# Two places for converted weights, and low parts kept in the raw buffer, in the first MoE of an attention kernel

## The chip, the cores and the metric

One core of one Trainium2 chip runs the whole program. The metric is the device time of one execution in microseconds (us); the kernel before takes 2153.35 us, the median of three runs (2152.96 to 2153.58). The engines are TensorE (PE, its weight loads PEld), VectorE (DVE), ScalarE (ACT), GpSimd (POOL) and SyncE (SP), which issues all the DMAs here. Each engine works through its own instructions in the order in which the program gave them out, and waits on semaphores for the others.

## The reference, cut to what matters

Attention with random features gives 2304 tokens of 512 numbers. They go through a first MoE (three weight matrices), and its result through a second with eight experts:

```python
g = x @ w_gate                       # 512 x 1536
silu = g * (1.0 / (1.0 + np.exp(-g)))
val = x @ w_val                      # 512 x 1536
x = (silu * val @ w_out)             # 1536 x 512
...
for e in range(E):                   # second MoE: w1[e] 512 x 1024, w2[e] 1024 x 512
    h = np.maximum(x @ w1[e], 0.0)
    out += P[:, e:e + 1] * (h @ w2[e])
```

The three weight matrices of the first MoE arrive as 64-bit floats, everything else as 32-bit floats. A product keeps its precision by splitting both factors in a high part (a rounded copy) and a low part (the rest), with three matmuls: high times high, high times low, low times high.

## The kernel before, in words

The program has three stages that matter here: attention (to 178 us), the first MoE (178 to 668 us), the second MoE (the rest).

**First MoE** (`moe1`). Six groups `g` of 256 hidden columns; in each, six steps `b` of 384 tokens. A step gives out `hunit(g, b, 0)`, then `ounit` of the step before, then `hunit(g, b, 1)`: 24 matmuls each (L707 to L709 in hunit, L739 to L741 in ounit), 72 in a step. At its end a hunit turns its two PSUM banks into the high and low part that the ounit will multiply: ACT silu (L717), DVE product (L718), ACT rounded copy (L721), DVE rest (L722). An ounit adds its four banks into an accumulator on DVE (L746).

**Weight tasks** (`m1_task`). The weights of group g+1 are made beside the matmuls of group g by six tasks, two for each matrix. A task is a generator: `pump(1)` runs it to its next `yield`, so that its instructions lie between those of the matmuls. Before the change a task has these pieces: ACT makes a float of the low word (L183); DVE has five operations on 32-bit words (L185, L187, L189, L191, L193) with two scratch halves of the tile `cv`, `a` and `s`; POOL multiplies (L195) and adds (L197); after an empty piece ACT makes the high part (L200) and POOL the low part (L202). That is 11 pieces. The load of a later task (L167 or L171, 512 KB, on SP) follows when the next pump finds the task at its end; it writes the raw buffer that the finished task has read. A step calls `pump(1)` ten times: three in each hunit, four in the ounit. After the ounit of a group's first step, `flush` runs whatever is left of the six tasks in one go, and the next six are put in the queue. From that queue's first pump to the flush there are 3 + 5 x 10 + 3 + 4 = 60 calls. The first six tasks run in the attention stage, at two pumps a step of its loop (L195 to L202 there too); L465 is the low part of the attention's input on DVE, L515 a matmul that reads it, and L436 the load of that input on SP.

**Sums** (`sums`). A second generator, `side`, makes sums of the second MoE's w2 blocks for later. It is called 14 times in a step: five times in each hunit, four in the ounit. For each of 32 blocks it loads 512 KB into one of two raw buffers (L306, SP), forms four sums on POOL in place (`subs`, L311 to L314), and for each half c makes a high part on ACT (L332, 128x512) and a low part on DVE (L338), and writes both to memory with four DMAs (L320, SP). Before the change there is one place for the high part and one for the low, `hl[0]` and `hl[1]`, so a half can be rounded only when the writes of the half before have landed. A block has 12 pieces; 14 pieces come ahead of the first block.

The generators give the order: nothing is moved about by a scheduler, and a semaphore wait stands wherever an instruction needs what another engine or a DMA has made, or writes what another still reads.

Of the kernel before, what the change touches and what calls it, by code (L numbers as in the profile page):

```python
# [11 lines left out]
F32 = mybir.dt.float32  # L12
F32R = mybir.dt.float32r
AF = mybir.ActivationFunctionType
ALU = mybir.AluOpType
# [5 lines left out]
P = 128  # L21
# [25 lines left out]
def f(ap):  # L47
    return ap.bitcast(F32)


class Kernel:
# [47 lines left out]
    def flush(self):  # L99
        while self.bg:  # L100
            self.pump(1000)

    def enqueue(self, n):
        for _ in range(n):
            self.bg.append(self.task(self.ntask))
            self.ntask += 1
# [28 lines left out]

    def make_tasks(self):
        self.tasks, self.raws, self.ntask, self.done = [], {}, 0, set()
        self.ahead, self.nload, self.tags, self.writes = 2, 0, deque((0, 1)), deque()
        for g in range(NG1):
            for which in range(3):  # L140
                for i in range(2):
                    self.tasks.append(self.m1_task(g, which, i))
        o = len(self.tasks) + 2
        for m in range(NG2):
            for q in range(2):
                self.tasks.append(self.w1_task(m, q))
            for i in range(2):
                self.tasks.append(self.w2_task(m, i))
        self.tasks.insert(o, self.tasks.pop(o + 2))
# [6 lines left out]
    def m1_task(self, g, which, i):  # L156
        nc = self.nc
        src = (self.wg, self.wv, self.wo)[which]
        dt, w = (F32, 1) if src.dtype == F32 else (I32, 2)
        if w == 2:  # L160
            src = src.bitcast(I32)
        src = src.rearrange("r (c w) -> r c w", w=w)

        def load(tag):
            if which < 2:
                t = self.raw.tile([P, 2, 256, w], dt, tag=tag, name=f"m1raw{g}_{which}_{i}")
                nc.sync.dma_start(t, src[i * 256:(i + 1) * 256, g * 256:(g + 1) * 256, :].rearrange("(c p) f w -> p c f w", p=P))  # L167
                return t.rearrange("p c f w -> p (c f) w")
            t = self.raw.tile([P, 512, w], dt, tag=tag, name=f"m1raw{g}_{which}_{i}")
            r0 = g * 256 + i * P  # L170
            nc.sync.dma_start(t, src[r0:r0 + P, :, :])  # L171
            return t

        def ops(t):
            hi, lo = [x.rearrange("p a b -> p (a b)")[:, i * 512:(i + 1) * 512] for x in self.m1_weights(g, which)]
            if dt == F32:
                x = t[:, :, 0]
            else:
                v = nc.vector
                w0, w1 = t[:, :, 0], t[:, :, 1]  # L180
                a, s = self.cv[:, 0:512], self.cv[:, 512:1024]
                x, y = f(a), t[:, :, 0].bitcast(F32)
                nc.scalar.activation(y, w0.bitcast(U32), AF.Copy, scale=2.0 ** -52)  # L183
                yield
                v.tensor_scalar(a, w1, 0x7FFFFFFF, None, op0=ALU.bitwise_and)  # L185
                yield
                v.tensor_scalar(x, x, F64_LO, F64_HI, op0=ALU.max, op1=ALU.min)  # L187
                yield
                v.tensor_scalar(a, a, 3, 0x3FFFFFF8, op0=ALU.logical_shift_left, op1=ALU.bitwise_and)  # L189
                yield  # L190
                v.scalar_tensor_tensor(a, w1, -0x40000000, a, op0=ALU.bitwise_and, op1=ALU.bitwise_or)  # L191
                yield
                v.tensor_scalar(s, a, -0x800000, None, op0=ALU.bitwise_and)  # L193
                yield
                nc.gpsimd.tensor_tensor(y, y, f(s), op=ALU.mult)  # L195
                yield
                nc.gpsimd.tensor_tensor(x, x, y, op=ALU.add)  # L197
                yield
                yield
            nc.scalar.copy(hi, x)  # L200
            yield
            nc.gpsimd.tensor_tensor(lo, x, f(hi), op=ALU.subtract)  # L202
            yield

        return load, ops, ("m1", g, which, i)


# [87 lines left out]

    def sums(self):
        nc, g_ = self.nc, self.nc.gpsimd
        hl = [self.ar2[:, 3072 + x * 512:3584 + x * 512] for x in range(2)]
        raws = [self.raw.tile([P, 2, 512], F32, tag="raw2", name="sumsraw"), self.cst.tile([P, 2, 512], F32, tag="ar2b", name="sumsraw2")]
        order = [(m, k) for m in range(NG2) for k in range(2)]  # L300

        def load(i):
            m, k = order[i]
            e, g = divmod(m, 2)
            r0 = g * 512 + k * 256
            nc.sync.dma_start(raws[i % 2], self.w2[e, r0:r0 + 256, :].rearrange("(c p) f -> p c f", p=P))  # L306

        def subs(i):
            t = raws[i % 2]
            a11, a21, a12, a22 = t[:, 0, 0:256], t[:, 0, 256:512], t[:, 1, 0:256], t[:, 1, 256:512]  # L310
            g_.tensor_tensor(a22, a21, a22, op=ALU.add)  # L311
            g_.tensor_tensor(a21, a11, a21, op=ALU.subtract)
            g_.tensor_tensor(a11, a22, a11, op=ALU.subtract)
            g_.tensor_tensor(a12, a12, a11, op=ALU.subtract)  # L314

        def write(i, c):
            m, k = order[i]
            for x in range(2):
                for j, n in enumerate(((6, 7), (3, 5))[c]):
                    nc.sync.dma_start(self.w2f[:, m, self.USE2.index(n), k, x, :], f(hl[x][:, j * 256:(j + 1) * 256]))  # L320

        load(0)
        for _ in range(8):
            yield
        subs(0)
        for _ in range(6):
            yield
        for i in range(len(order)):
            t = raws[i % 2]
            more = i + 1 < len(order)  # L330
            for c in range(2):
                nc.scalar.copy(hl[0], t[:, c, :])  # L332
                if c == 0 and more:
                    load(i + 1)
                yield
                if c and more:
                    subs(i + 1)
                nc.vector.tensor_tensor(hl[1], t[:, c, :], f(hl[0]), op=ALU.subtract)  # L338
                yield
                yield  # L340
                write(i, c)
                for _ in range(3):
                    yield

    def run(self):
        tc, nc = self.tc, self.nc
# [1162 lines left out]
```

## Time and profile before

| | |
|---|---|
| median of 3 runs | 2153.35 us (2152.96 to 2153.58) |
| the profiled execution | 2158.95 us, of which its span is 2157.2 us |
| PE busy | 2083.8 us, 97% of the span |
| DVE, POOL, ACT busy | 1361.2, 1055.9, 825.5 us (63%, 49%, 38%) |
| mean granted TensorE clock | 0.988 of full speed |
| read and written in memory | 337.89 and 125.35 MB |

The span runs from the first to the last instruction of one profiled execution. A busy share is a mean over all stages. A wait is idle time of an engine, put down to the semaphore event that came last before it ended. The granted clock is 1 at 2.4 GHz and 0.5 at 1.2 GHz.

### The profile page before, as it was taken

The numbers are of one execution on the slowest core, as the hardware profiler recorded it, in microseconds if no ns is written. First come the engines' busy times: TensorE is split into PE (matmuls) and PEld (weight loads), VectorE is DVE, ScalarE is ACT, GpSimd is POOL, SyncE is SP. The second block draws the span as 40 slices with busy tenths as digits, with TensorE's granted clock in tenths as the row PEclk, the third lists the DMA queues.
The fourth block names the chain that finished last, engine by engine and source line by source line (L and its number), as shares of the span: only waits on it lengthen the run. The fifth ranks groups of instructions, "written<-read, shape, count | busy, mean of one in ns | idle before, by whom it ended". The sixth has DMA issues, their size and how long they took to land.

```text
span 2157.2 us, 32509 instructions
## 1 busy us (share of the span) xinstructions
PE 2083.8 (97%) x11836; PEld 2008.9 (93%) x11836; DVE 1361.2 (63%) x2319; ACT 825.5 (38%) x1843; POOL 1055.9 (49%) x1049
## 2 busy tenths in 40 slices
PE   7999998998999999999999999999999999999998
PEld 7889998988999899899988999999998999999998
DVE  6996566666555654454445566666667566666666
ACT  6785433333244353344333433333233333333332
POOL 6774655555452454555454434434436434434433
PEclk9999999999999999999999999999999999999999
DMA  6542555555323567657667678877877778877784
GB/s 199 172 153 86 179 179 168 171 166 180 104 79 115 202 241 261 233 213 279 254 232 287 221 261 258 257 257 253 278 265 230 247 258 258 258 257 253 249 266 151
DMA packets 236752, 465.39 MB, mean 216 GB/s; under 512 B 20176, under 2 KB 108976, under 8 KB 232496
## 3 DMA queue, kind: packets, MB, share of 16 engines
q1 hardware_dynamic: 236592, 463.32, 63.9%
q8 instruction: 93, 1.52, 0.3%
q14 instruction: 67, 0.55, 0.1%
HBM read 337.89 MB, written 125.35 MB: 215 GB/s over the span
## 4 chain that ended last, share of the span: by engine, by line
PE 81%; DVE 8%; POOL 3%; ACT 3%; issue 2%; DMA 2%; SPq 0%; DVEq 0%; ACTq 0%; POOLq 0%
PE bank L1052 12%; PE pair L1383 7%; PE bank L1292 7%; PE bank L1294 7%; PE bank L1293 7%; PE pair L1385 7%; PE pair L1384 7%; PE bank L993 3%; PE bank L995 3%; PE bank L994 3%; PE bank L707 3%; PE bank L709 3%; PE bank L708 3%; DMA w2forms<-ar 2%; PE bank L739 2%
## 5 line engine op out<-in xcount | busy, mean ns | idle before, releaser
L1395 DVE TENSOR_TENSOR sums<-pair,sums 128x768 f32<-128x768 f32 x209 | 198.9, 952 | 46.2 <-PE pair L1385 46.1
L1292 PE MATMUL bank<-xh,ar 128*128 128x384 f32 x568 | 190.8, 336 | 4.4 <-DVE sums L1330 1.8
L1293 PE MATMUL bank<-xl,ar 128*128 128x384 f32 x568 | 190.3, 335 | 0.0
L1294 PE MATMUL bank<-xh,ar 128*128 128x384 f32 x568 | 190.3, 335 | 0.0
L1068 DVE SCALAR_TENSOR_TENSOR ac<-bank,mt,ac 128x512 f32<-128x512 f32 x84 | 63.1, 751 | 130.7 <-PE bank L1052 128.9
L195 POOL TENSOR_TENSOR m1raw<-m1raw,cv 128x512 f32<-128x512 f32 x36 | 49.6, 1378 | 171.2 <-issue 105.5
L1383 PE MATMUL pair<-xh,ar 128*128 128x384 f32 x342 | 115.0, 336 | 0.0
L1384 PE MATMUL pair<-xl,ar 128*128 128x384 f32 x342 | 114.6, 335 | 0.0
L1385 PE MATMUL pair<-xh,ar 128*128 128x384 f32 x342 | 114.6, 335 | 0.0
L1292 PEld LDWEIGHTS bank<-xh,ar 128*128 128x128 f32 x568 | 107.2, 189 | 5.7 <-DVE sums L1330 2.2
L1293 PEld LDWEIGHTS bank<-xl,ar 128*128 128x128 f32 x568 | 107.1, 189 | 0.0
L1294 PEld LDWEIGHTS bank<-xh,ar 128*128 128x128 f32 x568 | 107.1, 188 | 0.0
L718 DVE TENSOR_TENSOR mt<-bank,mt 128x384 f32<-128x384 f32 x72 | 40.0, 555 | 98.6 <-ACT mt L717 49.6
L707 PE MATMUL bank<-xh,ar 128*128 128x384 f32 x288 | 96.7, 336 | 0.0
L709 PE MATMUL bank<-xh,ar1b 128*128 128x384 f32 x288 | 96.2, 334 | 0.0
L709 PE MATMUL bank<-xh,ar 128*128 128x384 f32 x288 | 96.2, 334 | 0.0
L708 PE MATMUL bank<-xl,ar 128*128 128x384 f32 x288 | 96.2, 334 | 0.0
L707 PE MATMUL bank<-xh,ar1b 128*128 128x384 f32 x288 | 96.2, 334 | 0.0
L708 PE MATMUL bank<-xl,ar1b 128*128 128x384 f32 x288 | 96.2, 334 | 0.0
L993 PE MATMUL bank<-xh,ar 128*128 128x384 f32 x264 | 89.5, 339 | 6.5 <-DVE mt L1027 3.8
L535 ACT ACTIVATE at<-bank,bi 128x128 f32<-128x128 f32 x288 | 78.6, 395 | 43.1 <-DVE bi L528 36.0
L995 PE MATMUL bank<-xh,ar 128*128 128x384 f32 x264 | 89.0, 337 | 0.1
(382 smaller groups left out, 6958.2 us busy)
## 6 DMA issues: line engine op xcount, KB each, us to landing
ar<-w2forms SPq DMA_DIRECT2D x143, 512.0 KB, 4.5
ar<-w1forms SPq DMA_DIRECT2D x142, 512.0 KB, 4.9
w2forms<-ar SPq DMA_DIRECT2D x352, 128.0 KB, 2.9
ar1b<-w1forms SPq DMA_DIRECT2D x62, 512.0 KB, 4.9
ar1b<-w2forms SPq DMA_DIRECT2D x61, 512.0 KB, 4.4
w1forms<-ar SPq DMA_DIRECT2D x22, 1280.0 KB, 7.0
sumsraw<-in_w_dram SPq DMA_DIRECT2D x32, 512.0 KB, 4.5
w1raw<-in_w_dram SPq DMA_DIRECT2D x32, 512.0 KB, 4.3
```

The lines of the kernel that those rows point to most:

```text
L707: nc.tensor.matmul(t, hi[:, c, fs], self.xh[:, c, cs], start=(c == 0), stop=False)
L708: nc.tensor.matmul(t, hi[:, c, fs], self.xl[:, c, cs], start=False, stop=False)
L709: nc.tensor.matmul(t, lo[:, c, fs], self.xh[:, c, cs], start=False, stop=(c == KC - 1))
L993: nc.tensor.matmul(g, ah[:, c, :], bh[:, c, :], start=(first and c == 0), stop=False, skip_group_check=not first)
L1052: nc.tensor.matmul(y, a, w[:, fi % 2, ds], start=(first and x == 0 and k == 0 and fi == fis[0]), stop=(last and x == 1 and fi == fis[-1]))
L1292: nc.tensor.matmul(g, w[:, 0, d], bh[:, d, :], start=bool(first and d == 0), stop=False, skip_group_check=not first)
L1293: nc.tensor.matmul(g, w[:, 0, d], bl[:, d, :], start=False, stop=False, skip_group_check=not first)
L1294: nc.tensor.matmul(g, w[:, 1, d], bh[:, d, :], start=False, stop=(d == 1), skip_group_check=not first)
L1383: nc.tensor.matmul(y, w[:, k, 0, ds], h, start=(k == 0), stop=False)
L1384: nc.tensor.matmul(y, w[:, k, 0, ds], l, start=False, stop=False)
L1385: nc.tensor.matmul(y, w[:, k, 1, ds], h, start=False, stop=(k == 1))
L1395: v.tensor_tensor(a[n], pair, a[n], op=ALU.add)
```

## The change

Three things are changed. The weight tasks get two places for the converted value: `a` alternates between the halves of `cv`, and `s` goes into the raw buffer, over the high word that nothing reads any more. The split of a converted value (L200 and L202 before) leaves the task and becomes a generator of its own, `late`, which the next task runs: ACT's copy after the next task's L189, POOL's subtraction just ahead of its multiplication; `flush` runs what is left. The multiplication gets an empty piece behind it, and a task has 10 pieces instead of 11. In `sums`, the high parts get two places (one for each half c), the low parts are written over the raw values, and the order of a block's 13 pieces is: copy, subtract, next block's load, write; copy, subtract, empty, write; empty, the four sums of the next block, three empty.

```diff
     def flush(self):
         while self.bg:
             self.pump(1000)
+        for _ in self.late:
+            pass
...
+        def split(x):
+            hi, lo = [w.rearrange("p a b -> p (a b)")[:, i * 512:(i + 1) * 512] for w in self.m1_weights(g, which)]
+            nc.scalar.copy(hi, x)
+            yield
+            nc.gpsimd.tensor_tensor(lo, x, f(hi), op=ALU.subtract)
...
-                a, s = self.cv[:, 0:512], self.cv[:, 512:1024]
+                n = self.nconv % 2
+                self.nconv += 1
+                a, s = self.cv[:, n * 512:(n + 1) * 512], w1
...
                 v.tensor_scalar(a, a, 3, 0x3FFFFFF8, op0=ALU.logical_shift_left, op1=ALU.bitwise_and)
+                next(self.late, None)
                 yield
                 v.scalar_tensor_tensor(a, w1, -0x40000000, a, op0=ALU.bitwise_and, op1=ALU.bitwise_or)
                 yield
                 v.tensor_scalar(s, a, -0x800000, None, op0=ALU.bitwise_and)
                 yield
-                nc.gpsimd.tensor_tensor(y, y, f(s), op=ALU.mult)
+                for _ in self.late:
+                    pass
+                nc.gpsimd.tensor_tensor(y, y, s.bitcast(F32), op=ALU.mult)
+                yield
                 yield
                 nc.gpsimd.tensor_tensor(x, x, y, op=ALU.add)
-                yield
-                yield
-            nc.scalar.copy(hi, x)
-            yield
-            nc.gpsimd.tensor_tensor(lo, x, f(hi), op=ALU.subtract)
-            yield
+                self.late = split(x)
+                yield
+                yield
...
-        hl = [self.ar2[:, 3072 + x * 512:3584 + x * 512] for x in range(2)]
-        raws = [self.raw.tile([P, 2, 512], F32, tag="raw2", name="sumsraw"), self.cst.tile([P, 2, 512], F32, tag="ar2b", name="sumsraw2")]
+        his = [self.ar2[:, 3072 + x * 512:3584 + x * 512] for x in range(2)]
+        raws = [self.raw.tile([P, 2, 512], F32R, tag="raw2", name="sumsraw"), self.cst.tile([P, 2, 512], F32R, tag="ar2b", name="sumsraw2")]
+        lows, raws = raws, [f(r) for r in raws]
...
-            for x in range(2):
+            for x, w in enumerate((his[c], lows[i % 2][:, c, :])):
                 for j, n in enumerate(((6, 7), (3, 5))[c]):
-                    nc.sync.dma_start(self.w2f[:, m, self.USE2.index(n), k, x, :], f(hl[x][:, j * 256:(j + 1) * 256]))
+                    nc.sync.dma_start(self.w2f[:, m, self.USE2.index(n), k, x, :], f(w[:, j * 256:(j + 1) * 256]))
...
             for c in range(2):
-                nc.scalar.copy(hl[0], t[:, c, :])
+                nc.scalar.copy(his[c], t[:, c, :])
+                yield
+                nc.vector.tensor_tensor(lows[i % 2][:, c, :], t[:, c, :], f(his[c]), op=ALU.subtract)
+                yield
                 if c == 0 and more:
                     load(i + 1)
                 yield
-                if c and more:
-                    subs(i + 1)
-                nc.vector.tensor_tensor(hl[1], t[:, c, :], f(hl[0]), op=ALU.subtract)
-                yield
-                yield
                 write(i, c)
-                for _ in range(3):
-                    yield
+                yield
+            yield
+            if more:
+                subs(i + 1)
+            for _ in range(4):
+                yield
```

## Rows read from the trace of the kernel before

**Rows 1.** The page: the span, and busy time of each engine.
```profile
span 2157.2 us, 32509 instructions
PE 2083.8 (97%) x11836; PEld 2008.9 (93%) x11836; DVE 1361.2 (63%) x2319; ACT 825.5 (38%) x1843; POOL 1055.9 (49%) x1049
```

**Rows 2.** Stretches: length, busy PE, PEld, DVE, ACT, POOL (us), granted clock, DMA share, GB/s.
```profile
0.00:177.82 177.82, 153.91 (x1228) 147.36 (x1229) 153.03 (x343) 131.07 (x404) 126.91 (x169) 0.99 0.51 168
177.82:584.85 407.03, 386.89 (x2200) 381.34 (x2198) 257.61 (x434) 139.57 (x273) 220.97 (x212) 0.97 0.50 158
...
667.56:2157.20 1489.64, 1460.26 (x7936) 1398.63 (x7935) 903.99 (x1461) 522.77 (x1100) 676.06 (x644) 0.99 0.72 245
```

**Rows 3.** Same view: single steps of the first MoE, first to next hunit.
```profile
265.47:282.84 17.37, 14.48 (x73) 13.87 (x73) 10.33 (x16) 6.33 (x12) 10.63 (x12) 0.90 0.53 157
...
334.55:347.03 12.48, 12.48 (x74) 12.48 (x73) 9.08 (x16) 3.74 (x7) 7.85 (x8) 1.00 0.46 148
347.03:367.17 20.14, 15.37 (x74) 14.96 (x73) 11.24 (x17) 6.32 (x12) 13.36 (x14) 0.83 0.53 159
...
404.83:418.56 13.73, 13.03 (x73) 12.39 (x73) 10.14 (x18) 4.63 (x9) 7.78 (x8) 1.00 0.70 211
...
514.52:534.68 20.16, 15.17 (x73) 14.76 (x73) 11.04 (x17) 6.44 (x12) 13.24 (x13) 0.83 0.48 148
```

**Rows 4.** Waits of PE from 253 to 585 us: total, times, longest.
```profile
PE bank L739 <- ACT ar L721: 19.2, 7, 5.0
```

**Rows 5.** Timeline, 346 to 358 us: start, length, instruction, idle before it and releaser.
```profile
349.54 0.38 SPq L167 DMA_DIRECT2D m1raw<-in_gate_dram  x1
349.55 0.62 ACT L200 CAST ar<-cv 128x512 fp32r<-128x512 f32 x1 [6.59 <-POOL cv L197]
350.02 8.11 SPq L320 DMA_DIRECT2D w2forms<-ar  x7
...
354.44 0.62 ACT L332 CAST ar<-sumsraw 128x512 fp32r<-128x512 f32 x1 [3.71 <-DMA w2forms<-ar]
354.97 0.48 ACT L717 ACTIVATE mt<-bank 128x384 f32<-128x384 f32 x1
```

**Rows 6.** Busy time by stretch, straight behind the longest wait of that step.
```profile
356.64:362.30 5.66, 5.66 (x18) 5.57 (x19) 5.01 (x9) 1.37 (x3) 2.78 (x2) 0.50 0.46 135
```

**Rows 7.** Busy time: the second step of group 5, sums done, gating matmuls added.
```profile
597.33:611.22 13.89, 13.89 (x81) 13.89 (x81) 8.21 (x16) 7.71 (x16) 9.13 (x9) 1.00 0.20 64
```

**Rows 8.** Waits of ACT, then of SP, from 178 to 585 us.
```profile
ACT ar1b L200 <- POOL cv L197: 52.6, 13, 8.3
ACT ar L200 <- POOL cv L197: 46.4, 12, 8.3
ACT ar L332 <- DMA w2forms<-ar: 36.0, 21, 3.9
...
SPq L167 <- DVE cv L191: 23.2, 4, 6.1
```

**Rows 9.** Lines asked for singly: ns least/median/most; last two: landing of L320, L306.
```profile
L185 DVE TENSOR_SCALAR cv<-m1raw x36: 410/616/960, 23.8 to 591.4; 128x512 int32<-128x512 int32 x36
L191 DVE SCALAR_TENSOR_TENSOR cv<-m1raw,cv x36: 676/682/695, 31.1 to 593.8; 128x512 int32<-128x512 int32 x36
L193 DVE TENSOR_SCALAR cv<-cv x36: 410/417/430, 34.9 to 594.6; 128x512 int32<-128x512 int32 x36
L195 POOL TENSOR_TENSOR m1raw<-m1raw,cv x36: 1295/1302/1764, 35.5 to 595.1; 128x512 f32<-128x512 f32 x36
L338 DVE TENSOR_TENSOR ar<-sumsraw,ar x64: 678/1025/1756, 196.7 to 568.5; 128x512 fp32r<-128x512 f32 x64
...
DMA to landing us min/median/max: 1.7/2.2/4.8
DMA to landing us min/median/max: 3.6/4.5/5.8
```

**Rows 10.** POOL's groups from 178 to 585 us: busy us, mean ns.
```profile
L311 POOL TENSOR_TENSOR sumsraw<-sumsraw 128x256 f32<-128x256 f32 x31 | 28.6, 924 | 0.0
```

More of the change, by code (lines that the diff above doesn't have):

```diff
@@ L137, in make_tasks @@
         self.tasks, self.raws, self.ntask, self.done = [], {}, 0, set()
+        self.late, self.nconv = iter(()), 0
         self.ahead, self.nload, self.tags, self.writes = 2, 0, deque((0, 1)), deque()
@@ L172, in load @@
             return t
+        def split(x):
[3 more added lines that the diff above has]
+            nc.gpsimd.tensor_tensor(lo, x, f(hi), op=ALU.subtract)
         def ops(t):
-            hi, lo = [x.rearrange("p a b -> p (a b)")[:, i * 512:(i + 1) * 512] for x in self.m1_weights(g, which)]
             if dt == F32:
                 x = t[:, :, 0]
+                yield from split(x)
+                yield
             else:
@@ L335, in sums @@
                 yield
-                if c and more:
-                    subs(i + 1)
-                nc.vector.tensor_tensor(hl[1], t[:, c, :], f(hl[0]), op=ALU.subtract)
+                write(i, c)
                 yield
+            yield
+            if more:
+                subs(i + 1)
+            for _ in range(4):
                 yield
-                write(i, c)
-                for _ in range(3):
-                    yield
     def run(self):
```

## The prediction

> **What bounds the kernel now.** First the page: PE is busy for 2083.8 of 2157.2 us [rows 1], so a change that leaves the matmuls alone can only win back PE's idle time and time at a lower clock. Next the stretches, to find the stage: the change touches groups 0 to 4 of the first MoE, 407.0 us with a granted clock of 0.97, and six tasks in attention; the 1489.6 us behind the first MoE hold none of it [rows 2]. Then single steps. An undisturbed step takes 12.48 us, PE busy throughout [rows 3]; 30 of them would take 374.4 us, so 407.03 - 374.4 = 32.6 us are lost here. They are lost in a pattern: the second step of groups 1 to 4 takes 17.4 to 20.2 us (four steps, of which three stand in the rows, 17.37, 20.14 and 20.16), and the sixth step of groups 1 to 3 about 14 us (three steps, one in the rows, 13.73) [rows 3]. PE's waits name the releaser: 19.2 us in seven waits for ACT's rounded copy L721 [rows 4]. That is less than 32.6, since the clock falls after the idle time: the 5.66 us behind the longest wait of one such step ran at 0.50, the 1.2 GHz level [rows 6]. Idle time and half clock go together; what removes one removes the other.
>
> Why L721 is late stands in the timeline of one such step [rows 5]. ACT first sits 6.59 us before L200, the split of the sixth task, because POOL's addition L197 is given out just ahead of it in the flush. It then sits 3.71 us before L332, because the one place for a high part is still being written out: that write was issued at 350.02, behind the load L167 at 349.54, which SP held until L197 had read the raw buffer. Only then comes the silu L717, at 354.97. Both waits are common: 99.0 us in 25 waits before L200 and 36.0 us in 21 before L332 [rows 8]. Most cost nothing, because the silu behind them was not due.
>
> **The change, part by part.** *The flush.* A task had 11 pieces, so six had 66; 60 pumps come before the flush, which gave out the last 6 pieces at once. Now six tasks have exactly 60 pieces, and only the last split is left. Each task now lies alike in its step: L183, L185, L187 in the second hunit, L189, L191, L193 in the next first hunit, the multiplication and the addition in the ounit. I take away the burst.
>
> *The split.* ACT's copy comes five pumps after the addition instead of two, that is a second hunit (4.16 us, a third of 12.48) and more later. POOL then needs its subtraction, multiplication and addition, 3 x 1.3 = 3.9 us [rows 9], perhaps four sums first, 4 x 0.92 = 3.7 us [rows 10]; I let them start 3.5 us into a step: DVE is done with the unit before some 2 us in (my estimate for silu to rest, four operations of about 0.5 us, as L717 takes 0.48 [rows 5]), and L189 to L193 take 1.5 us [rows 9]. The addition then ends 7 to 11 us into the step, and the copy is due after 12.5. The 99 us before L200 should nearly go. In the flush the last split still follows its addition closely, but ACT's next silu is due only at about 10.5 us of that step and is needed at 16.6, where the next step's ounit starts. So it has cover of some 5 us; without cover it would cost what a step costs now.
>
> *DVE's wait.* L185 no longer waits for the subtraction of the task before, since `a` has two places. Cover: DVE is busy 257.6 of 407 us here [rows 2].
>
> *`s` in the raw buffer.* L193 now writes every second word. No row shows a strided write. Below: 0.41 us, as L185 takes at its least with a strided read; above: 0.69 us, as L191 takes with one [rows 9]. I take 0.42, since L185 is the nearest form. The upper end adds 36 x 0.27 = 9.7 us of DVE work, hidden in the MoE, and 6 x 0.27 = 1.6 us in attention, where DVE is busy 153 of 177.8 us [rows 2]. POOL's multiplication reads `s` strided: it already reads and writes a strided word at 1.30 us, and 1.76 was its most [rows 9]; 0 to 36 x 0.46 = 16.6 us of POOL, which is busy 221 of 407. I take 0; a gain is excluded in both, the amount of data being the same.
>
> *The sums.* With two places the copy L332 waits for the write of two halves before, long landed, and ACT's 36 us before L332 go. In return, a raw buffer is read by two DMAs until they land, so the load L306 waits on SP for a landing (median 2.2 us, at most 4.8 [rows 9]) where it waited for DVE. Behind it on SP stand the next writes and a task's load; who waits for it is POOL with the four sums, and ACT with the copy four side calls behind them. From a block's last subtraction to the copy that needs the buffer anew there are 21 side calls, 21 x 12.48/14 = 18.7 us. Against that: four writes issued (1.7 us at 0.42, L320's median), landing 2.2, load 4.5 [rows 9], sums 3.7 [rows 10], together 12.1 us; with the longest landing and load 16.0 us. It fits, so I cost it at nothing. A block has 13 pieces instead of 12. The last write is call 14 + 31 x 13 + 8 = 425; until the sums are finished off in group 5 there are 10 + 29 x 14 + 9 = 425 calls. No burst is left there either.
>
> *Attention.* Same operations, 10 pieces per task instead of 11, so each falls always in the same half of a step. DVE, ACT and POOL are all loaded (153, 131, 127 of 177.8 us [rows 2]). I see no reason for a sign and take 0, with 4 us either way: six tasks at 0.7 us, about half a POOL operation.
>
> **The sum.** 32.6 us go, nothing comes. Made against the profiled execution: 2158.95 - 32.6 = 2126.3 us. The median stands 5.6 us below that execution, so 2153.35 - 32.6 = 2120.7, say **2121 us**. A row that speaks for it: in group 5, where the sums were done, the same flush cost no idle time at all (13.89 us, PE busy for 13.89, the gating matmuls included [rows 7]).
>
> **The rivals.** *A, the boundary stall stays in part.* The copy L332 now follows its sums by four calls instead of five, and sums still run in the flush steps; if POOL is late there, ACT waits for POOL where it waited for the DMA, and the silu stays behind. Half the loss of those four steps, (17.4 + 20.1 + 20.2 + 19 - 4 x 12.48)/2 = 13 us, would remain (the step without a row taken at 19): 2134 us. For it: L332's wait was the last to end [rows 5]. Against it: 7.5 us of POOL work fit in a step, and clean steps with sums exist.
>
> *B, slower: the sums' chain becomes the bound.* If SP is held by a task's load, as it was for up to 6.1 us [rows 8], the 16.0 us become 22.1 against 18.7 and some 2.4 us that the silu can wait: 1 us over. From 22.2 us on, over 30 blocks, the 32.6 us are eaten up (1.1 us each). At 24 us it would be 30 x 2.9 = 87 us lost, 2153 + 87 - 33 = 2207 us. Against it: SP's long waits came from loads given out while the task was still being converted, and 22 us takes every part at its worst at once.
>
> *C, attention pays.* POOL and DVE stretch each other: L338, least 0.68, had a median of 1.03 us, and L195 went from 1.30 to 1.76 [rows 9]. The change puts a task's subtraction and multiplication back to back, close to L191 and L193; at 0.46 us more for three POOL operations in six tasks, 8.3 us are lost: 2129 us. The Trainium skill (GPSIMD Engine Reference, Specifications) says that GpSimd's SBUF interfaces are shared with VectorE, with contention from two-input and two-port instructions there; by that rule this loss comes whenever the two lie side by side, and the stretched rows agree.
>
> *D, no change.* The lost time would have to come back whole, in attention or behind; no row suggests it.
>
> **How the numbers follow.** The forecast has 0.85: 2114 to 2128, from 4 us of attention either way and about 3 us for clock drops that fall differently. A has 0.06, B 0.02, C 0.05, D 0.02. The range reaches up to take in C and most of a milder A: 2114 to 2131. A measurement of this kernel can tell about 0.2%, 4.3 us, from no change. Forecast, A and C are faster by more than that: 0.96; D 0.02; B 0.02.
>
> **What would show it.** In the trace after: steps 2 and 6 of groups 1 to 4 at 12.5 us; PE's wait for L721 gone; ACT's waits before the split's copy and the sums' copy near 0; a granted clock of 1.00 from 178 to 585 us; that stretch near 375 us, attention within 4 us of 178. The forecast is wrong if ACT waits for POOL before the sums' copy and PE behind it (A), if SP waits long before L306 (B), or if the attention stretch grows (C).

## The result, and the profile after

The changed kernel takes 2123.55 us (median of 4 runs, 2121.67 to 2129.94), the kernel before 2153.47 in the same comparison. The ratio is 0.986, with a 95% interval of 0.9843 to 0.9877: some 30 us, 1.4%, faster. The forecast was 2121, the range 2114 to 2131.

The page after: the span, and the busy time of each engine (to be read beside [rows 1]):

```profile
span 2119.9 us, 32594 instructions
PE 2065.5 (97%) x11836; PEld 1994.6 (94%) x11836; DVE 1396.1 (66%) x2319; ACT 825.1 (39%) x1843; POOL 1058.2 (50%) x1049
```

The same stretches as in [rows 2], in the kernel after (length, busy PE, PEld, DVE, ACT, POOL, granted clock, DMA share, GB/s):

```profile
0.00:177.06 177.06, 151.83 (x1229) 144.67 (x1229) 151.63 (x344) 131.18 (x404) 122.24 (x164) 0.96 0.53 168
177.06:552.60 375.54, 375.23 (x2199) 374.23 (x2198) 291.74 (x434) 138.52 (x272) 227.24 (x217) 1.00 0.55 169
635.31:2119.90 1484.59, 1455.71 (x7937) 1394.14 (x7935) 904.97 (x1461) 522.64 (x1100) 677.37 (x644) 0.99 0.73 246
```

Groups 0 to 4 went from 407.03 to 375.54 us, 31.5 us less, at a granted clock of 1.00. PE is idle there for 0.3 us. Attention is 0.8 us shorter, and group 5 the same 82.71 us. The span fell by 37.3 us, so 5.0 us are left: they lie behind the first MoE (1489.64 to 1484.59 us), where nothing was changed; PE's busy time there is 4.6 us shorter for the same matmuls, so they ran faster, and hardly less was waited. At least half of it is scatter between executions: a second profile of the same kernel (below) took 1487.1 us there. Counted from the end of the first MoE's last matmul, that part took 1474.4 to 1479.4 us in the eleven profiles of this case, and a run with the changed tasks (the second one below) took as long there as the kernel before. The medians, not the two spans, tell what the change gives.

Single steps after, the second of groups 1 and 2, the sixth of group 2, and the second of group 4 (to be read beside [rows 3]):

```profile
264.73:277.21 12.48, 12.48 (x74) 12.48 (x73) 9.87 (x16) 3.75 (x7) 6.72 (x7) 1.00 0.79 247
339.61:352.09 12.48, 12.48 (x74) 12.48 (x73) 10.31 (x18) 3.54 (x7) 7.58 (x9) 1.00 0.74 221
389.53:402.01 12.48, 12.48 (x74) 12.48 (x73) 9.34 (x15) 4.09 (x8) 7.59 (x7) 1.00 0.65 202
489.37:502.68 13.31, 13.00 (x73) 12.39 (x73) 10.53 (x16) 5.58 (x11) 8.32 (x9) 1.00 0.63 195
```

Of these four, all but one are down to 12.48 us. PE's waits from 253 to 553 us are one line, for the step that took 13.31 (beside it [rows 4]; L755 and L737 are the L739 and L721 of before):

```profile
PE bank L755 <- ACT ar L737: 0.3, 1, 0.3
```

What ACT waits for in groups 0 to 4 has changed its nature ([rows 8]; L179 is the split's copy, L346 the sums'):

```profile
ACT ar L346 <- POOL sumsraw L327: 32.3, 12, 3.7
ACT ar L179 <- POOL cv L213: 5.6, 2, 4.3
...
ACT ar L346 <- DMA w2forms<-sumsraw: 2.0, 1, 2.0
ACT ar1b L179 <- POOL cv L213: 1.3, 1, 1.3
```

The 99.0 us before the split are 6.9, and the 36.0 us for landed writes are 2.0; instead ACT waits 32.3 us for POOL's sums. SP waits instead. L320, the sums' load, stands until the writes from its raw buffer have landed; L170, a task's load, stands until POOL's addition has read the buffer that it fills:

```profile
SPq L320 <- DMA w2forms<-sumsraw: 46.7, 30, 4.5
...
SPq L170 <- POOL cv L213: 27.4, 8, 7.3
```

Of all this only the 0.3 us above reach PE. So the time is where the forecast looked for it. Whether the reasons hold is another matter: the change has several parts, and the next runs take them apart.

### The profile page after: what moved, and what is told of

Its sections match the earlier page's. It is cut to its first block, busy times and chain, and to the rows that moved or that the text cites. A ratio compares the mean times of both kernels' runs of the same rounds, so it can differ in the third digit from the quotient of the medians.

```text
span 2119.9 us, 32594 instructions
## 1 busy us (share of the span) xinstructions
PE 2065.5 (97%) x11836; PEld 1994.6 (94%) x11836; DVE 1396.1 (66%) x2319; ACT 825.1 (39%) x1843; POOL 1058.2 (50%) x1049
## 4 chain that ended last, share of the span: by engine, by line
PE 89%; DVE 7%; POOL 1%; issue 1%; DMA 1%; ACT 1%; SPq 0%; DVEq 0%; POOLq 0%; ACTq 0%
PE bank L1068 12%; PE pair L1399 7%; PE bank L1308 7%; PE bank L1309 7%; PE bank L1310 7%; PE pair L1400 7%; PE pair L1401 7%; PE bank L724 4%; PE bank L723 4%; PE bank L725 4%; PE bank L1009 4%; PE bank L1011 3%; PE bank L1010 3%; PE bank L755 2%; PE bank L757 2%; PE bank L756 2%
## 5 line engine op out<-in xcount | busy, mean ns | idle before, releaser
L1309 PE MATMUL bank<-xl,ar 128*128 128x384 f32 x568 | 190.2, 335 | 0.0
L737 ACT CAST ar<-mt 128x384 fp32r<-128x384 f32 x72 | 37.0, 514 | 172.4 <-DVE mt L734 172.4
L724 PE MATMUL bank<-xl,ar 128*128 128x384 f32 x288 | 96.3, 334 | 0.0
L1010 PE MATMUL bank<-xl,ar 128*128 128x384 f32 x264 | 88.7, 336 | 0.0
```

The costliest lines, as they stand in the source:

```text
L724: nc.tensor.matmul(t, hi[:, c, fs], self.xl[:, c, cs], start=False, stop=False)
L1309: nc.tensor.matmul(g, w[:, 0, d], bl[:, d, :], start=False, stop=False, skip_group_check=not first)
```

## The experiments

Each ratio below is to the kernel before on the same chip, with its 95% interval. Two numbers are read from each trace beside it: the length of groups 0 to 4 (407.0 us before, 375.5 after), and PE's waits at the starts of the groups.

**The changed kernel again** (no edit).

> The changed kernel once more, on the chip of the three runs beside it. Theory M (the change takes away two waits in a row on ACT, and nothing else of weight): the 30 steps of groups 0 to 4 take 374 to 376 us again, the first MoE is the same in each profile, and what differs between executions lies behind 640 us, in where the clock falls to 1.2 GHz; median 2121 to 2126 us. Rival V (the gain itself varies, since a step has little slack): another profile has several steps over 13 us and the boundary waits of PE come back, 2126 to 2135 us.

Ratio 0.9858 (0.9838 to 0.9877), median 2125.67 us (2120.76 to 2127.72). Groups 0 to 4 took 376.0 us, with two steps of 13.0 and 13.3 us. The gain in the MoE stands; what differs between executions is attention (177.9 us) and the part behind. V is out.

**The tasks changed, the sums as before.** Against the changed kernel:

```diff
-        his = [self.ar2[:, 3072 + x * 512:3584 + x * 512] for x in range(2)]
+        hl = [self.ar2[:, 3072 + x * 512:3584 + x * 512] for x in range(2)]
...
```

> The weight tasks of the changed kernel with the sums of the kernel before (one place each for high and low, 12 pieces). Theory M: the burst is gone, ACT does not sit before the split, and SP's load of raw weights is not held while the sums' write stands behind it, so the wait for the landed write shrinks too; at least 28 of the 31 us are won, 2121 to 2127 us, groups 0 to 4 at 374 to 379 us. Rival P (the sums' places are what counts, since the wait before the sums' copy ended last): ACT still waits for landings at the boundary, PE waits 2 to 4 us there four times, 2138 to 2150 us.

Ratio 0.9937 (0.9914 to 0.996), 2143.29 us; groups 0 to 4 took 389.7 us. M expected at least 28 us; the stage gave 17.3, the medians 11.8. Rival P's range held, and its signs too: PE waited once at each of the four starts, 1.75 to 2.5 us. The timeline at the start of group 2 (start, length, instruction, idle before it; the step began at 336.03) shows why:

```profile
348.42 0.38 SPq L170 DMA_DIRECT2D m1raw<-in_gate_dram  x1
348.43 0.62 ACT L179 CAST ar<-cv 128x512 fp32r<-128x512 f32 x1 [1.29 <-POOL cv L213]
348.91 8.20 SPq L333 DMA_DIRECT2D w2forms<-ar  x7
...
353.42 0.62 ACT L345 CAST ar<-sumsraw 128x512 fp32r<-128x512 f32 x1 [3.79 <-DMA w2forms<-ar]
353.95 0.48 ACT L730 ACTIVATE mt<-bank 128x384 f32<-128x384 f32 x1
```

The split waits only 1.29 us now, but SP's load still stands until the addition ends, at 348.4, 12.4 us into the step, and the sums' write behind it. ACT waits 3.79 us for the landing as before, and the silu comes at 353.95, 17.9 us into the step.

**The sums changed, the tasks as before.** Against the kernel before:

```diff
-        hl = [self.ar2[:, 3072 + x * 512:3584 + x * 512] for x in range(2)]
+        his = [self.ar2[:, 3072 + x * 512:3584 + x * 512] for x in range(2)]
...
```

> The sums of the changed kernel (two places for high parts, low parts in the raw buffer, 13 pieces) with the weight tasks of the kernel before (66 pieces, a burst of 6 in the flush). Theory M: ACT still sits 6 us before the split at each boundary, and then waits for POOL's sums instead of the landing where they fall there; half of the loss stays or a little more, 2132 to 2148 us, with PE's waits at the boundaries of 1 to 4 us. Rival P: with the second wait gone the silu comes some 4 us earlier, PE's longest wait of 5.0 us shrinks under 1 us and no clock drop follows, 2121 to 2129 us.

Ratio 0.9957 (0.9941 to 0.9974), 2145.6 us; groups 0 to 4 took 392.0 us. That is M's range and not P's, and ACT still sat 5.48 us before the split. What came behind it was not the wait for POOL's sums that M named: here a wait of DVE shows that had been hidden behind the two others (the start of group 2, from 327.69):

```profile
342.06 0.62 ACT L200 CAST ar<-cv 128x512 fp32r<-128x512 f32 x1 [5.48 <-POOL cv L197]
...
343.15 0.60 ACT L333 CAST ar<-sumsraw 128x512 fp32r<-128x512 f32 x1
...
343.66 0.49 ACT L720 ACTIVATE mt<-bank 128x384 f32<-128x384 f32 x1
...
344.08 0.94 DVE L185 TENSOR_SCALAR cv<-m1raw 128x512 int32<-128x512 int32 x1 [4.87 <-POOL ar L202]
...
344.95 1.21 DVE L335 TENSOR_TENSOR sumsraw<-sumsraw,ar 128x512 fp32r<-128x512 f32 x1
...
346.08 0.94 DVE L187 TENSOR_SCALAR cv<-cv 128x512 f32<-128x512 f32 x1
...
346.94 0.55 DVE L721 TENSOR_TENSOR mt<-bank,mt 128x384 f32<-128x384 f32 x1
...
348.08 0.69 PE L742 MATMUL bank<-ar,ar 128*128 128x384 f32 x1 [3.07 <-ACT ar L724]
```

ACT does not wait before L333 at all. The silu L720 is done by 344.15, but the product L721 runs at 346.94: in DVE's order it stands behind L185, which waited 4.87 us for POOL's subtraction to free the one place of the converted value, and behind L335 and L187, both slowed by POOL's sums. This run also tests the forecast's reading of [rows 7]: with 13 pieces a block the sums last into group 5, and its second step, clean before, now has idle time and a granted clock of 0.83 (PE busy 17.00 of 20.52 us):

```profile
578.98:599.50 20.52, 17.00 (x82) 16.55 (x81) 10.65 (x22) 7.86 (x16) 11.11 (x10) 0.83 0.19 61
```

**Eleven pieces again** in the changed kernel.

```diff
                 self.late = split(x)
                 yield
                 yield
+                yield
```

> The changed kernel with one more empty piece at the end of each weight task, so that six tasks have 66 pieces for 60 pumps and the flush gives out the last 6 at once, the last split among them. Theory M: what counts is that ACT waits for POOL at the boundary longer than its 5 us of cover; the last task's multiplication, addition and split in one burst make ACT wait some 4 to 6 us, so a loss of 0 to 2 us at each of four boundaries, 2123 to 2132 us. Rival F (the burst alone makes the loss): the second steps of groups 1 to 4 are back at 17 us or more, 2140 to 2150 us.

Ratio 0.9889 (0.9868 to 0.9909), 2130.67 us; groups 0 to 4 took 380.8 us, PE waited 2.9 us in four waits, 1.1 at most. M was right, F was not: with all the places, the burst costs 5 us, not 30.

**The changed sums and two places in the tasks**, split and 66 pieces as before. Against the run with the changed sums alone:

```diff
-                a, s = self.cv[:, 0:512], self.cv[:, 512:1024]
+                n = self.nconv % 2
+                self.nconv += 1
+                a, s = self.cv[:, n * 512:(n + 1) * 512], w1
...
```

> The run with the changed sums alone, plus two places for the converted value in the weight tasks (a alternates, s in the raw buffer); the split stays at the end of its own task, with 66 pieces and the burst. Theory M2 (three waits at a boundary, of which the slowest counts: ACT before the split, ACT before the sums' copy, DVE before the next task's first operation for POOL's subtraction): only the first is left, and it ends about 1 us before PE needs the result; groups 0 to 4 take 374 to 382 us, 2122 to 2133 us. Rival L (the late split is what counts; the places of the tasks do little): as with the changed sums alone, 2138 to 2147 us, PE's boundary waits still 1.4 to 3.6 us.

Ratio 0.9915 (0.9897 to 0.9933), 2136.88 us. The time fits neither range as a whole. The stage took 382.3 us, the upper end of M2's, and 9.7 less than with the changed sums alone. So the two places are worth 10 us once ACT's second wait is gone. Not all of that is DVE's wait: POOL's multiplication is shorter with them (next run), and at the start of group 2 the rounded copy ends 2.23 us earlier, of which 0.69 come from an earlier silu and 1.54 from DVE's order (table below). That the median lies above 2133 comes from group 5, whose second step still stalls (17.76 us instead of 13.89), and from what scatters outside.

**Two places in the tasks alone** (the edit above, on the kernel before).

> The kernel before with two places for the converted value alone (a alternates, s in the raw buffer), split, pieces and sums as before. Theory M2: DVE's waits for POOL's subtraction go, ACT's two remain, and the silu is as late as before; groups 0 to 4 lose 26 to 33 us, 2147 to 2156 us. Rival D (DVE's wait ahead of the product is the main one): half of the loss goes, 2136 to 2144 us. Beside it, POOL's multiplication: 1.04 us if reading s from the raw buffer is what shortens it, 1.30 us if not.

Ratio 0.9968 (0.9956 to 0.998), 2147.93 us; groups 0 to 4 took 401.3 us, PE waited 16.4 us at L742. M2's range held: with ACT's two waits in place, DVE's is worth nothing at the start of group 2, where the copy ended 1.62 us behind the silu's start with it and without it. Most of the 5.7 us won came another way. POOL's multiplication took 1.04 us instead of 1.30, and the last additions ended 0.5 to 0.6 us earlier in all four groups (14.41 us into the step instead of 14.96 in group 2), with the silu and PE's wait behind them.

**One place for the high part** in the changed kernel.

```diff
-        his = [self.ar2[:, 3072 + x * 512:3584 + x * 512] for x in range(2)]
+        his = [self.ar2[:, 3072:3584] for x in range(2)]
```

> The changed kernel with one place for the sums' high part instead of two, all else as changed. The copy of the second half follows the write of the first by one side call, 0.9 us, where landing takes about 3 us. Theory M2: ACT waits for landings some 2 to 4 us in every block, which is covered within a step but not at the boundaries, where SP holds the writes behind a task's load; PE waits 1 to 4 us at most boundaries, 2126 to 2142 us. Rival S (with the flush mended the silu has slack enough): 2120 to 2127 us.

Ratio 0.9973 (0.9964 to 0.9983), 2149.59 us, worse than either theory said: nearly the whole gain is gone. PE waited four times, but not where M2 looked: 8.3 us in the sixth step of group 1 and 8.8 us in the first of group 4.

```profile
PE bank L755 <- ACT ar L737: 19.0, 4, 8.8
```

With the new order of the block the copy of the second half follows the first half's write at once, and ACT waited 75.3 us for landings (20 waits, up to 7.8). In the sixth step of group 1 the first half's write was issued only at 320.83 us, behind a task's load that SP held until POOL's addition ended at 319.85; ACT's copy stood 7.77 us for it, to 326.96, and the silu behind it. That is M2's mechanism, at a place where it did not look. The second place is what the new order of the sums stands on.

**Ten pieces** in the kernel before, nothing else.

```diff
                 nc.gpsimd.tensor_tensor(x, x, y, op=ALU.add)
                 yield
-                yield
             nc.scalar.copy(hi, x)
```

> The kernel before with one empty piece less in each weight task, so that six tasks have 60 pieces for 60 pumps; one place for everything, split at the end of its own task. Theory M2: no burst, but the split now stands one pump behind its addition, and the three waits are still there; half or more of the loss stays, 2135 to 2152 us. Rival F (the burst alone): the boundary stalls go, 2121 to 2130 us.

Ratio 0.9861 (0.9842 to 0.988), 2125.78 us. M2 was wrong and F right about the time: one empty piece less, with one place for everything, gives what the whole change gives. Groups 0 to 4, and the second step of group 2 (20.14 us before):

```profile
177.60:554.60 377.00, 376.22 (x2199) 374.12 (x2198) 260.58 (x436) 140.67 (x274) 224.77 (x213) 1.00 0.55 172
340.62:353.35 12.73, 12.73 (x74) 12.44 (x73) 9.23 (x16) 4.82 (x10) 7.02 (x8) 1.00 0.58 195
```

The waits themselves are still there, at the start of group 2 (from 327.82):

```profile
338.03 0.62 ACT L199 CAST ar<-cv 128x512 fp32r<-128x512 f32 x1 [1.53 <-POOL cv L197]
...
342.96 0.62 ACT L331 CAST ar<-sumsraw 128x512 fp32r<-128x512 f32 x1 [3.73 <-DMA w2forms<-ar]
343.49 0.48 ACT L716 ACTIVATE mt<-bank 128x384 f32<-128x384 f32 x1
```

ACT waits as long for the landing as in [rows 5], 3.73 us, and from 178 to 560 us it still waits 53.1 us before the split and 30.5 for landings; but the whole chain lies 5 us earlier, since the addition L197 ended at 338.0, 10.2 us into the step, instead of 15.0. The silu at 15.7 us is just in time; in group 4 it comes at 16.3, and PE waits 0.7 us, its only wait here.

**What the boundary obeys.** For the step at the start of group 2, in us from its start, read from the timelines of each run:

| kernel | addition ends | silu of the second unit | its product on DVE | rounded copy (L721) ends | PE waits |
|---|---|---|---|---|---|
| before | 14.97 | 20.42 | 20.94 | 22.04 | 4.77 |
| tasks changed | 12.36 | 17.91 | 18.43 | 19.53 | 2.26 |
| sums changed | 14.35 | 15.97 | 19.26 | 20.35 | 3.07 |
| eleven pieces | 13.90 | 15.53 | 17.27 | 18.37 | 1.27 |
| sums and places | 13.65 | 15.28 | 17.03 | 18.12 | 1.02 |
| ten pieces | 10.18 | 15.67 | 16.18 | 17.29 | 0.00 |
| changed kernel | 10.20 | 11.84 | 14.47 | 15.56 | 0.00 |

In each row that waits (the fourth and fifth as the sum of two waits), PE's wait is the end of the rounded copy less 17.1 to 17.3 us. What counts at this place is one moment: the copy must end by about 17.3 us (the forecast had put it at 16.6). On the way to it stand the addition's end, then ACT's wait for a landing (from the addition's end to the silu 5.4 to 5.6 us with one place for the high part, 1.6 with two), then DVE's backlog. An edit that brings the sum under 17.3 clears this step, and one that takes off a part wins that part. It says nothing of the other steps: with one place for the high part in the changed kernel the copy of this step ended at 17.17 us and PE did not wait for it, but 8.3 us were waited one step earlier and 8.8 in group 4.

**Everything together**: the changed sums, two places, ten pieces, the split at the end of its own task. Against the changed kernel:

```diff
...
                 nc.gpsimd.tensor_tensor(y, y, s.bitcast(F32), op=ALU.mult)
                 yield
-                yield
                 nc.gpsimd.tensor_tensor(x, x, y, op=ALU.add)
-                self.late = split(x)
                 yield
-                yield
+            nc.scalar.copy(hi, x)
+            yield
+            nc.gpsimd.tensor_tensor(lo, x, f(hi), op=ALU.subtract)
+            yield
...
```

> The changed sums, two places for the converted value, and tasks of 10 pieces that keep their split at their own end: no burst, no landing wait, no split left over for the flush. Theory M3 (PE waits at a boundary as far as ACT's silu of the step's second unit starts later than about 15.3 us into the step; that time is the end of the last addition plus what ACT then waits for): the addition ends 9 to 11 us in, the silu starts at 11 to 13, so no boundary waits; groups 0 to 4 lose under 1.5 us, 2120 to 2127 us, the same as the changed kernel within 0.2%. Rival L (the late split is needed to keep POOL and ACT apart in the other steps): losses of 5 us and more come back in third and sixth steps, 2127 to 2135 us.

Ratio 0.9859 (0.9843 to 0.9875), 2123.09 us. M3's range held and PE's waits went; the four additions end even earlier than it said, 6.5 to 9.4 us into their steps, the silus start at 10.7 to 12.7, and PE never waits in groups 0 to 4:

```profile
175.21:549.92 374.71, 374.71 (x2199) 374.32 (x2198) 266.13 (x434) 141.28 (x272) 215.57 (x213) 1.00 0.54 170
```

It is not measurably faster than the changed kernel or the ten pieces alone (the intervals lie over one another), but it has the most slack: the last 0.8 us of the changed kernel are gone, and DVE is busy for 266 us instead of 292.

## Why the prediction was right, point by point

*The bound and the sum.* 32.6 us were to go, 31.5 went. Idle time and half clock went together. This was a count of lost time and not of parts, and it would have come out for any edit that clears these steps. That this one does was in part luck: the copy due by 17.3 us ended at 13.9, 15.6, 13.9 and 17.6 in groups 1 to 4, and two of the terms below were wrong.

*The flush.* Right, and more than the forecast saw: it listed the 60 pieces as one part of several. In the kernel before they are enough alone; in the changed kernel, with all its places, they are worth some 5 us (eleven pieces).

*The split.* The direction was right (99 us of waits became 6.9), the size off: the last addition was put at 7 to 11 us into the step. It came at 8.3, 10.2, 7.8 and 14.0 in groups 1 to 4. In the last, POOL's sums stood 6.64 us for a load that SP had issued late, at 477.52, behind a task's load that had waited for the addition before, and the subtraction and the multiplication stood behind them; ACT waited 4.33 us, and 5 us of cover were just too few, by 0.3 us:

```profile
483.56 0.74 POOL L325 TENSOR_TENSOR sumsraw<-sumsraw 128x256 f32<-128x256 f32 x1 [6.64 <-DMA sumsraw<-in_w_dram]
...
490.92 0.62 ACT L179 CAST ar<-cv 128x512 fp32r<-128x512 f32 x1 [4.33 <-POOL cv L213]
...
492.52 0.48 ACT L733 ACTIVATE mt<-bank 128x384 f32<-128x384 f32 x1
```

*DVE's wait.* Costed at nothing, under cover of a busy share. That step was wrong, though the sum did not show it, since the change takes the wait away: at the boundary L185 stands ahead of the product, and once the silu is early the two places are worth 10 us (sums changed against sums and places), some two thirds of it by DVE's order at the step that the table shows. A busy share over 407 us says nothing of one place in the order.

*`s` in the raw buffer.* DVE's strided write cost next to nothing: L206 (L193 before) has a median of 428 ns against 417. For POOL's multiplication a gain was excluded, the amount of data being the same, and there was one: 1.04 us against 1.30. It brings the last addition forward, and is most of the 5.7 us that the two places win alone.

*The sums.* The landing waits went. The chain from a block's last subtraction to the end of the sums that use the buffer anew stayed under 18.7 us in 27 of 30 blocks and took 19.3 to 20.7 in three. SP's own wait for landings was within what the forecast allowed (up to 4.5 us, against 4.8). What the sum left out was the task's load, held by POOL's addition up to 7.3 us: behind it the sums' load was issued 7.0 to 12.0 us after the subtraction, in seven blocks. So the beginning of rival B's mechanism came, without its loss. Rival A's came too, 32.3 us of ACT waiting for POOL, and found slack everywhere but in group 4.

*Attention.* 177.82 to 177.06 us says little: the same attention program as before took 174.6 us in one run, the changed one 181.4 in another. The 4 us put on it were about right. *Rival C's* stretching took place, but in the MoE: DVE's busy time rose from 257.6 to 291.7 us there, under cover (the last section has the operation). D did not come.

## What to carry to other kernels

In an order written out by hand, look for the moment by which a result must be there, and add up the waits that stand in series before it; the wait that ends last is only the last of them, and each is worth what it brings the sum closer to that moment, and nothing beyond it. Before giving out more buffers, count whether the background work fits into its slots: a generator one empty piece too long had made the burst that brought these waits past their moment, and without it most of them were still there and cost nearly nothing. And a wait is not covered by an engine's mean idle time if something urgent stands behind it in that engine's order.

## What the hardware did that was not expected

POOL's multiplication of 128x512 words got faster when its second factor moved into the raw buffer, where the words of both factors alternate: 1.04 us in the median of 36 in the run with two places alone, which changed nothing else for it, against 1.30 with the factor in a tile of its own (from the line asked for, ns least, median, most):

```profile
L198 POOL TENSOR_TENSOR m1raw<-m1raw x36: 1041/1043/1500, 35.5 to 591.5; 128x512 f32<-128x512 f32 x36
```

A DVE operation with two inputs took longer beside a POOL operation that had begun before it. L204, in groups 0 to 4 and a little behind them, took 691 to 693 ns in the 12 cases with no POOL operation beside it (682 in the median before, as L191, [rows 9]). In the other 18 a POOL operation had begun first, the split's subtraction L181 in all but one; L204 then took 1.10 to 1.78 us, and ended 0.55 us behind the end of the POOL operation each time, while the subtraction, some 1.29 us alone, took 1.47 to 1.56 us beside it. In the last run above, where the split keeps to its own task, four cases began ahead of one of POOL's sums: they kept their 691 to 693 ns, and the sum ended 0.59 to 0.60 us behind them; a fifth began behind a sum and took 1.28 us. So here the one that began first lost little, and the other ended behind it. Why is not shown.

```profile
L204 DVE SCALAR_TENSOR_TENSOR cv<-m1raw,cv 128x512 int32<-128x512 int32 x30 | 38.1, 1269 | 0.9
```
